# Linear attention with a gated feed-forward block: order of the first two token tiles' projections, and of the last tile's drains

## The chip, the cores and the metric

The kernel runs on one core of a Trainium2 chip. The metric is the device time of one execution in microseconds (us). The core's engines run their own instruction streams and wait for each other by semaphores: TensorE (PE in the profile, with its weight loads as PEld), VectorE (DVE), ScalarE (ACT), GpSimd (POOL), and SyncE (SP), which here issues the DMA transfers.

## The reference

For a sequence of S=2048 tokens of width D=576, with F=4608 and 32 heads of 18:

```python
def _A_ref(x, wqkv, wo):
    qkv = (x @ wqkv).reshape(B, S, 3, H, Dh).transpose(2, 0, 3, 1, 4)
    phi = lambda t: where(t > 0, t + 1, exp(t)) + 1e-6
    pq, pk = phi(q), phi(k)
    kv = einsum("bhsd,bhse->bhde", pk, v)
    z = einsum("bhsd->bhd", pk)
    o = einsum("bhqd,bhde->bhqe", pq, kv) / (einsum("bhqd,bhd->bhq", pq, z)[..., None] + 1e-6)
    return merge_heads(o) @ wo
xn = layernorm(x)
s = _A_ref(xn, wqkv, wo)
g = silu(gelu(xn @ w1 + b1) @ w2 + b2)
return x + s * g
```

All inputs are f32, and the kernel keeps f32 accuracy: every operand of a large product is split into a high part in the matmul's type (fp32r) and the low part that is left, and three products (high by high, high by low, low by high) are added.

## The kernel before

**Tiles.** 2048 tokens are 16 tiles of 128. The first phase handles them in pairs `(p, s)`: p is the pair, s its first or second tile. Pair 0 is called x8 and x12 here, after the names of the tiles, pair 1's first tile is `(1, 0)`. Each tile is loaded (`load_x`, L239), its mean and variance taken (`x_stats`, L244: two `bn_stats`, an aggregation and an addition on VectorE, a power on POOL, and, where ScalarE is to normalise, one more product on VectorE and on POOL), normalised (`x_norm`, L258: on ScalarE, or with `on_vector` on VectorE), and transposed by TensorE in five blocks into one PSUM buffer `pt` (`transpose_x`, L273). From there it is split: `x_hi` (L282, ScalarE casts it into `xH`, or for s=1 also into `x_tmp0h`/`x_tmp1h`), `x_lo` and `x_lo_tmp` (L293, L304: VectorE subtracts, into `xL` and `x_tmp0l`), and a raw copy is kept for later (`x_raw`, L290, ScalarE, into `rt` or `scr`).

**Weights.** The columns of `wqkv` for keys (1) and values (2) come in five slices of the contraction, k=0 to 4, of 288 KB each (`raw_w`, L533); slice 4, the rest, has 64 rows that are used as high and low part together. `Weight.split_k` (L159) lets ScalarE cast a slice to its high part and the engine that it is given (DV for VectorE, GP for POOL) subtract for the low part; `split_rest` and `split_v` do so for the rest and for the values.

**A projection.** `Plain` (L388) makes keys or values of one tile: 14 pairs of matmuls (each pair covers 2 x 288 columns): for k=0 to 3 the products number 3k (high by high), 3k+1 (low weights), 3k+2 (low x), and for the rest 12 and 13. `part(a, b)` issues a stretch of them. When the last is issued, ScalarE drains the two PSUM banks. K8 stands for the keys of x8, V8 for its values, and so on; in the profile both have the line L411 and the output `pl`, and their weights are `wkq_h`, `wkq_l`, `wkq_rh`, `wkq_rl` for keys, `wv_h`, `wv_l` for values.

**Order.** The start (L541 to L600) is recorded under `in_order()`, so each engine executes its instructions in the order in which they are written. The later pairs follow a plan of numbered times (`plan_pair`, L613), then come the projections that share sums of two tiles, the attention output, and the feed-forward phase. TensorE begins with 20 warm-up transposes (L453). Before, the order of projections is K8, V8, K12, V12. DMA issues go through SyncE's queue in written order.

**The tail.** `down_plain` (L1393) makes the last product of the feed-forward phase for the tiles 0 to 7 of the last group. Tiles 6 and 7 are halved by columns (`pd6a`, `pd6b`, `pd7a`, `pd7b`). Each half is drained by VectorE (`macc`, L1403), goes through silu on ScalarE (L1404), is multiplied (`xs`, L1356) and added to x (L1357), and stored. For tile 6's second half POOL does the last two, else VectorE.

Of the kernel before, what the change touches and what calls it, by code (L numbers as in the profile page):

```python
# [42 lines left out]
def linear_attention_gated_ffn(ctx, tc, x, wqkv, wo, w1, b1, w2, b2, out):  # L43
    nc = tc.nc
# [199 lines left out]
    def x_stats(p, s, first=False):  # L244
# [3 lines left out]
        nc.vector.bn_stats(st[:, 1, :], raw[:, HD:])  # L248
        mv = t1.tile([P, 4], F32, tag="mv", name=f"mv{p}{s}")
        nc.vector.bn_aggr(mv[:, 0:2], st)  # L250
        nc.vector.tensor_scalar_add(mv[:, 2:3], mv[:, 1:2], 1e-5)
        nc.gpsimd.tensor_tensor(mv[:, 3:4], mv[:, 2:3], nhalf, op=ALU.pow)
# [3 lines left out]
        stats[p, s] = mv  # L256

    def x_norm(p, s, on_vector=False):  # L258
        mv, raw = stats.pop((p, s)), xraw.pop((p, s))
# [128 lines left out]
    class Plain:  # L388


        def __init__(self, p, s, wk, dst, bias):
            cs = pair_cols(p)
            if s == 0:
                xk = [(xH[:, k, cs], xL[:, k, cs]) for k in range(4)] + [(xH[:, 4, cs],)]
            else:
                h, l = x_tmps[p % 2]
                xk = [(h[:, k], l[:, k]) for k in range(2)]
                xk += [(xH[:, 5 + k, cs], xL[:, 4 + k, cs]) for k in range(2)] + [(xH[:, 7, cs],)]
            self.seq = []
            for k in range(KT):  # L400
                h, l = xk[k][0], xk[k][-1]
                self.seq += [(h, 0, k), (h, 1, k)] + ([(l, 0, k)] if k < 4 else [])
            self.wk, self.dst, self.bias = wk, dst, bias
            self.ps = [bank(f"pl{p}{s}{n}")[:, :HD] for n in range(2)]

# [22 lines left out]
    def wv_part(hl, k, n):  # L428
        return (wv_h, wv_l)[hl][:, k, n * HD : (n + 1) * HD]

    def plain_k(p, s):
        return Plain(p, s, wk_part, k_ts[p % 2][s], one)

    def plain_v(p, s):
        return Plain(p, s, wv_part, v_t[s], None)
# [97 lines left out]
    def raw_w(which, between=None):  # L533
        raw, rest = w2p.tile([P, CF * D], F32, tag="w2r", name=f"raw{which}"), stage(D, f"rr{which}")
        for k in range(KT):
            dst = rest if k == 4 else raw[:, k * D : (k + 1) * D]
            nc.sync.dma_start(dst, wqkv[k, :, which * D : (which + 1) * D])
            if k == 2 and between:
                between()
        return raw, rest  # L540

    DV, GP = nc.vector, nc.gpsimd
    kt_raw = lambda raw, k: raw[:, k * D : (k + 1) * D]
    load_x(0, 0)
    raw_k, rest_k = raw_w(1, lambda: load_x(0, 1))
    x_stats(0, 0, True), x_norm(0, 0, True)
    wkq.split_k(0, kt_raw(raw_k, 0), DV)
    wkq.split_k(1, kt_raw(raw_k, 1), GP)
    transpose_x(0, 0)
    cs = pair_cols(0)  # L550
    nc.vector.tensor_copy(xH[:, 0:2, cs], pts[0, 0][:, 0:2])
    nc.vector.tensor_copy(xH[:, 2:5, cs], pts[0, 0][:, 2:])
    x_lo(0, 0)
    wkq.split_k(2, kt_raw(raw_k, 2), GP)
    wkq.split_k(3, kt_raw(raw_k, 3), DV)
    wkq.split_rest(rest_k, GP)
    raw_v, rest_v = raw_w(2, lambda: load_x(1, 0))
    load_x(1, 1)
    x_stats(0, 1, True), x_norm(0, 1, True)
    x_raw(0, 0)  # L560
    nc.gpsimd.memset(zacc, 0.0)

    N14 = 14
    plain_k(0, 0).part(0, N14)
    transpose_x(0, 1)
    split_v(0, kt_raw(raw_v, 0), DV)
    split_v(1, kt_raw(raw_v, 1), GP)
    x_hi(0, 1), x_lo_tmp(0), x_lo(0, 1)
    split_v(2, kt_raw(raw_v, 2), DV)
    split_v(3, kt_raw(raw_v, 3), GP)  # L570
    split_v(4, rest_v, DV)
    load_x(2, 0)
    load_x(2, 1)
    plain_v(0, 0).part(0, N14)
    x_stats(1, 0)
    x_raw(0, 1)
# [14 lines left out]
    s_hi(0), s_lo(0)  # L591
    x_store(0)
    plain_v(0, 1).part(0, N14)
    phi_exp(k_t[1], e_t[1])
    transpose_x(1, 1)
    x_hi(1, 1), x_lo_tmp(1), x_lo(1, 1)
    x_norm(2, 0)
# [754 lines left out]
        pair, src = tails["hs", b, f]  # L1352
        set_lo(pair, src, nc.vector)

    def gate_part(t, c, xt, s_t, cs, eng):
        eng.tensor_tensor(s_t[:, cs], c[:, cs], s_t[:, cs], op=MUL)  # L1356
        eng.tensor_tensor(s_t[:, cs], s_t[:, cs], xt[:, cs], op=ADD)  # L1357
        nc.sync.dma_start(out[t * P : (t + 1) * P, cs], s_t[:, cs])

# [33 lines left out]
    def down_plain(t, ws):  # L1393
# [226 lines left out]
```

## Time and profile before

| what | value |
|---|---|
| median of three runs | 1117.99 us (1117.21 to 1118.75) |
| the profiled execution, its own time | 1118.17 us |
| its span in the trace | 1116.4 us, 18757 instructions |
| TensorE busy | 1095.4 us, 98% of the span |
| VectorE, ScalarE, POOL busy | 812.6, 504.2, 466.1 us |
| granted TensorE clock, mean | 1.00 |
| DMA | 271.92 MB, mean 244 GB/s |
| first projection matmul | at 7.74 us |
| transposes of tile (1,0) | at 23.02 us |
| last matmuls begin | at 1109.85 us, for 0.56 |

The profile gives, in its rows, the start or the busy time of instructions by engine and line (L411 is line 411 of the kernel before), the output and the input of the operation, and behind them how long the engine sat idle and which engine's result ended it. A busy TensorE is not TensorE at its peak; the granted clock is given beside it in the windows.

### The profile page before, as it was taken

What the parts mean: (1) busy time and instruction counts of PE and PEld (TensorE: products, weight loads), DVE (VectorE), ACT (ScalarE), POOL (GpSimd) and SP (SyncE); (2) the same over time, 40 slices, a digit from 0 to 9 for tenths busy, and PEclk for the clock granted to TensorE, in tenths of its full rate; (3) what the DMA queues carried; (4) which work ended last, traced back from release to release, by engine and by line L of the source; (5) the groups of instructions that cost most, each with busy time, mean ns of one, the idle gap of its engine ahead of it and who ended that gap; (6) DMA issues with size and microseconds to landing.
All of it is one profiled execution on the core that took longest, in us unless ns stands there. A gap on an engine that the chain in (4) does not pass through costs nothing.

```text
span 1116.4 us, 18757 instructions
## 1 busy us (share of the span) xinstructions
PE 1095.4 (98%) x6924; PEld 1014.2 (91%) x6924; DVE 812.6 (73%) x1242; ACT 504.2 (45%) x913; POOL 466.1 (42%) x419
## 2 busy tenths in 40 slices
PE   8999999999999999999999999999999999999997
PEld 7899999999898898988989889899898998988987
DVE  6877667877688888888888887666475574664766
ACT  6766555554544444454443544424233243242351
POOL 5854433655354353543535433323224133242340
PEclk9999999999999999999999999999999999999999
DMA  5888747785988879588796869978766666766243
GB/s 203 301 261 280 253 135 224 250 285 188 358 270 308 265 236 355 177 296 272 229 357 185 288 235 382 359 252 282 225 204 213 214 200 216 226 200 218 85 142 114
DMA packets 95531, 271.92 MB, mean 244 GB/s; under 512 B 10381, under 2 KB 21133, under 8 KB 93391
## 3 DMA queue, kind: packets, MB, share of 16 engines
q1 hardware_dynamic: 90543, 260.68, 66.2%
q0 software_dynamic: 4896, 10.03, 5.3%
q8 instruction: 55, 0.90, 0.3%
q14 instruction: 37, 0.30, 0.1%
HBM read 165.94 MB, written 100.01 MB: 238 GB/s over the span
## 4 chain that ended last, share of the span: by engine, by line
PE 88%; DVE 4%; DMA 3%; ACT 2%; issue 1%; POOL 1%; SPq 0%; DVEq 0%; POOLq 0%; ACTq 0%
PE pm L1287 30%; PE e L1147 12%; PE a L1147 10%; PE zy L1147 10%; PE pl L411 5%; PE ps_s L894 5%; PE b L1147 4%; PE e L356 2%; DMA xH<-x_dram 2%; PE a L356 2%; PE z L356 2%; PE pd L1410 2%; PE ps_kva L464 1%; PE b L356 1%; DVE h_l L924 1%
## 5 line engine op out<-in xcount | busy, mean ns | idle before, releaser
L921 ACT CAST h_h<-g 128x512 fp32r<-128x512 f32 x204 | 120.1, 621 | 138.9 <-PE pm L1287 137.8
L924 DVE TENSOR_TENSOR h_l<-g,h_h 128x512 fp32r<-128x512 f32 x204 | 159.5, 782 | 0.0
L1295 DVE TENSOR_TENSOR macc<-macc,pm 128x576 f32<-128x576 f32 x128 | 96.2, 751 | 37.7 <-PE pm L1287 36.0
L1254 POOL TENSOR_TENSOR mid<-g 128x512 f32<-128x512 f32 x34 | 43.9, 1292 | 181.6 <-ACT g L1155 181.6
L1147 PE MATMUL a<-xH,wa 128*128 128x512 f32 x360 | 117.2, 390 | 0.5 <-DMA xH<-x_dram 0.5
L1297 DVE TENSOR_TENSOR macc<-pm,macc 128x576 f32<-128x576 f32 x90 | 68.2, 757 | 25.4 <-PE pm L1287 24.4
L1155 ACT ACTIVATE g<-b,b1c 128x512 f32<-128x512 f32 x36 | 24.8, 688 | 125.0 <-DVE b L1173 125.0
L1147 PEld LDWEIGHTS a<-xH,wa 128*128 128x128 f32 x360 | 67.6, 188 | 14.4 <-DMA xH<-x_dram 0.7
L1147 PE MATMUL e<-xSH,wb 128*128 128x512 f32 x216 | 66.6, 390 | 0.2 <-DVE b L1173 0.2
L1164 ACT COPY mid<-a 128x512 f32<-128x512 f32 x36 | 21.2, 588 | 91.2 <-PE a L1147 91.1
L1248 POOL TENSOR_TENSOR g<-g 128x512 f32<-128x512 f32 x34 | 49.5, 1456 | 22.2 <-DVE h_l L924 20.9
L1381 POOL TENSOR_TENSOR fin1l<-fin1h,fin1l 128x288 f32<-128x288 f32 x8 | 6.4, 805 | 121.9 <-DMA fin1l<-s_dram 63.0
L1147 PE MATMUL a<-xL,wa 128*128 128x512 f32 x144 | 56.2, 390 | 0.0
L1251 POOL TENSOR_TENSOR g<-g 128x512 f32<-128x512 f32 x34 | 49.9, 1467 | 13.1 <-DVE h_l L924 11.8
L1167 DVE TENSOR_TENSOR mid<-b,mid 128x512 f32<-128x512 f32 x36 | 24.6, 685 | 37.5 <-PE b L1147 37.4
L1147 PE MATMUL b<-xSH,w 128*128 128x512 f32 x144 | 50.2, 389 | 0.0
L1147 PE MATMUL zy<-xSH,w 128*128 128x512 f32 x144 | 50.2, 389 | 0.0
L1147 PE MATMUL e<-xSH,w 128*128 128x512 f32 x144 | 50.2, 389 | 0.0
L1147 PE MATMUL zy<-xH,w 128*128 128x512 f32 x144 | 50.2, 389 | 0.0
L1147 PEld LDWEIGHTS e<-xSH,wb 128*128 128x128 f32 x216 | 40.5, 188 | 9.0 <-DVE b L1173 0.6
L1245 POOL TENSOR_TENSOR g<-g 128x512 f32<-128x512 f32 x34 | 47.1, 1386 | 2.7
L1155 ACT ACTIVATE g<-e,b1c 128x512 f32<-128x512 f32 x36 | 24.8, 688 | 49.2 <-DVE e L1180 49.2
(932 smaller groups left out, 3594.2 us busy)
## 6 DMA issues: line engine op xcount, KB each, us to landing
op<-w SPq DMA_DIRECT2D x72, 256.0 KB
w<-op SPq DMA_DIRECT2D x72, 256.0 KB
w1raw<-w SPq DMA_DIRECT2D x18, 640.0 KB
w2raw<-w SPq DMA_DIRECT2D x10, 1152.0 KB
op_a<-wa SPq DMA_DIRECT2D x18, 640.0 KB
wa<-op_a SPq DMA_DIRECT2D x18, 640.0 KB
op<-w2o SPq DMA_DIRECT2D x19, 576.0 KB
w2r<-w SPq DMA_DIRECT2D x6, 1152.0 KB
```

Of the source, the lines that this page charges most:

```text
L356: nc.tensor.matmul(ps, st, mv, start=first and n == 0, stop=n == len(seq) - 1, skip_group_check=True,)
L411: nc.tensor.matmul(self.ps[n], st, self.wk(hl, k, n), start=(i == 0), stop=(i == n_all - 1))
L894: nc.tensor.matmul(self.ps[h], st[:, k, :], w[:, k, h * HD : (h + 1) * HD], start=(i == 0), stop=(i == len(self.seq) - 1),)
L921: nc.scalar.copy(pair[0], src)
L924: eng.tensor_tensor(pair[1], src, pair[0].bitcast(F32), op=SUB)
L1147: nc.tensor.matmul(ps.rearrange("p (c j) -> p c j", c=4), st, mv, start=first and n == 0, stop=n == len(seq) - 1, skip_group_check=True,)
L1155: nc.scalar.activation(g, ps, AF.Gelu_apprx_tanh, bias=b1c[:, f : f + 1])
L1248: tt(src[6, pr], src[5, pr], A(0, 0), op=ADD)
L1251: tt(src[3, pr], src[6, pr], A(0, 1), op=SUB)
L1287: nc.tensor.matmul(ps[:, q, :HD], hs[p][st][:, cs], m[:, p, :], start=(n == 0 and i not in CHAIN), stop=(n == len(seq) - 1), skip_group_ch ...
L1295: nc.vector.tensor_tensor(dst, dst, src, op=SUB)
L1297: nc.vector.tensor_tensor(dst, src, dst, op=ADD)
```

## The change

The sequence of the first two tiles is written anew, and in the tail the last tile's two halves are interleaved. No matmul is added or removed.

Loads: x12 is now the second transfer, ahead of all weights; the value slices and the tiles of pair 1 follow in the order of before. `x_stats` is divided in `x_bn` and `x_rstd`. x12 is normalised on ScalarE instead of VectorE, and with it come the one product on VectorE and the one on POOL. The first `xH` cast of slices 2 to 4 goes from VectorE to ScalarE; the low parts of k0 and k3 go from VectorE to POOL, those of k2 and the rest from POOL to VectorE. Projections come as K8, K12, V8, V12. K8 takes its 14 pairs in the order `FIRST`, and x12's transposes stand between its ninth and tenth pair; K12 takes them in the order `LATE`, with low x last. The exponential of tile 12's keys is issued before V12 instead of behind it.

```diff
-    def __init__(self, p, s, wk, dst, bias):
+    def __init__(self, p, s, wk, dst, bias, order=range(14)):
...
+        self.seq = [self.seq[i] for i in order]
...
+    FIRST = (0, 3, 2, 5, 6, 1, 8, 9, 4, 11, 7, 12, 10, 13)
+    LATE = (0, 1, 3, 4, 6, 7, 9, 10, 12, 13, 2, 5, 8, 11)
+    N14 = 14
     load_x(0, 0)
-    raw_k, rest_k = raw_w(1, lambda: load_x(0, 1))
-    x_stats(0, 0, True), x_norm(0, 0, True)
-    wkq.split_k(0, kt_raw(raw_k, 0), DV)
-    wkq.split_k(1, kt_raw(raw_k, 1), GP)
+    load_x(0, 1)
+    raw_k, rest_k = raw_w(1)
+    raw_v, rest_v = raw_w(2, lambda: load_x(1, 0))
+    load_x(1, 1)
+    x_bn(0, 0), x_rstd(0, 0, True)
+    x_bn(0, 1)
+    x_norm(0, 0, True)
+    x_rstd(0, 1)
+    wkq.split_k(0, kt_raw(raw_k, 0), GP)
     transpose_x(0, 0)
     cs = pair_cols(0)
     nc.vector.tensor_copy(xH[:, 0:2, cs], pts[0, 0][:, 0:2])
-    nc.vector.tensor_copy(xH[:, 2:5, cs], pts[0, 0][:, 2:])
+    wkq.split_k(1, kt_raw(raw_k, 1), GP)
+    nc.scalar.copy(xH[:, 2:5, cs], pts[0, 0][:, 2:])
     x_lo(0, 0)
-    wkq.split_k(2, kt_raw(raw_k, 2), GP)
-    wkq.split_k(3, kt_raw(raw_k, 3), DV)
-    wkq.split_rest(rest_k, GP)
-    raw_v, rest_v = raw_w(2, lambda: load_x(1, 0))
-    load_x(1, 1)
-    x_stats(0, 1, True), x_norm(0, 1, True)
+    x_norm(0, 1)
+    wkq.split_k(2, kt_raw(raw_k, 2), DV)
     x_raw(0, 0)
+    wkq.split_k(3, kt_raw(raw_k, 3), GP)
+    wkq.split_rest(rest_k, DV)
     nc.gpsimd.memset(zacc, 0.0)
-    N14 = 14
-    plain_k(0, 0).part(0, N14)
+    pr = plain_k(0, 0, FIRST)
+    pr.part(0, 9)
     transpose_x(0, 1)
+    x_hi(0, 1), x_lo_tmp(0), x_lo(0, 1)
     split_v(0, kt_raw(raw_v, 0), DV)
     split_v(1, kt_raw(raw_v, 1), GP)
-    x_hi(0, 1), x_lo_tmp(0), x_lo(0, 1)
+    pr.part(9, N14)
     split_v(2, kt_raw(raw_v, 2), DV)
     split_v(3, kt_raw(raw_v, 3), GP)
+    x_stats(1, 0)
+    plain_k(0, 1, LATE).part(0, N14)
     split_v(4, rest_v, DV)
     load_x(2, 0)
     load_x(2, 1)
-    plain_v(0, 0).part(0, N14)
-    x_stats(1, 0)
     x_raw(0, 1)
     for i in (3, 2, 1, 5, 4):
         x_sum(0, i, GP, xf(0, 1))
     k_t = k_ts[0]
     phi_exp(k_t[0], e_t[0])
     x_norm(1, 0)
-    plain_k(0, 1).part(0, N14)
+    plain_v(0, 0).part(0, N14)
+    phi_exp(k_t[1], e_t[1])
     transpose_x(1, 0)
...
     plain_v(0, 1).part(0, N14)
-    phi_exp(k_t[1], e_t[1])
     transpose_x(1, 1)
...
-        for k in range(2):
-            drain(k)
-            gate_part(*part(k))
+        drain(0), gate_mul(*part(0))
+        if t == 6:
+            gate_add(*part(0))
+        drain(1)
+        if t > 6:
+            gate_add(*part(0))
+        gate_mul(*part(1)), gate_add(*part(1))
```

In the last lines `gate_part` has been divided in `gate_mul` (the product) and `gate_add` (the sum and the store); tile 6 keeps its order.

ScalarE's order at the start, before (a name's number is that of its buffer; `raw_168` are the key slices, `raw_207` and `rr_208` the values', `pt_191` and `pt_262` the transposes of x8 and x12):

```order
L156 CAST wkq_h<-raw_168 128x2x288 x4
L167 CAST wkq_rh<-rr_169 128x576
L291 COPY rt<-pt_191 128x640
L420 ACTIVATE k_162<-pl_230,c_84 128x288
L420 ACTIVATE k_162<-pl_231,c_84 128x288
L438 CAST wv_h<-raw_207 128x576 x2
L287 CAST xH<-pt_262 128x384
L288 CAST x_tmp0h<-pt_262 128x256
L438 CAST wv_h<-raw_207 128x576 x2
L438 CAST wv_h<-rr_208 128x576
```

and with the change (`raw_170`, `raw_177`, `pt_209`, `pt_252` in the same roles; `xn_221` is x12 normalised):

```order
L156 CAST wkq_h<-raw_170 128x2x288 x2
L569 CAST xH<-pt_209 128x384
L274 ACTIVATE xn_221<-x_168,mv_201 128x576
L274 ACTIVATE xn_221<-x_168,mv_201 128x64
L156 CAST wkq_h<-raw_170 128x2x288
L298 COPY rt<-pt_209 128x640
L156 CAST wkq_h<-raw_170 128x2x288
L167 CAST wkq_rh<-rr_171 128x576
L294 CAST xH<-pt_252 128x384
L295 CAST x_tmp0h<-pt_252 128x256
L446 CAST wv_h<-raw_177 128x576 x2
```

The cast of xH's second part and x12's normalisation now stand between the casts of k1 and k2, the copy `rt` between k2 and k3, and x12's casts ahead of K8's drain.

VectorE's order in the same place, before (`mv` holds a tile's statistics):

```order
L264 TENSOR_SCALAR xn_184<-x_166,mv_180 128x576
L264 TENSOR_SCALAR xn_184<-x_166,mv_180 128x64
L157 TENSOR_TENSOR wkq_l<-raw_168,wkq_h 128x2x288
L551 CAST xH<-pt_191 128x256
L552 CAST xH<-pt_191 128x384
L297 TENSOR_TENSOR xL<-pt_191,xH 128x512
L301 TENSOR_TENSOR xH<-pt_191,xH 64x128
L157 TENSOR_TENSOR wkq_l<-raw_168,wkq_h 128x2x288
```

and with the change:

```order
L247 BN_STATS st_195<-x_168 128x6
L248 BN_STATS st_195<-x_168 128x6
L271 TENSOR_SCALAR xn_198<-x_166,mv_191 128x576
L271 TENSOR_SCALAR xn_198<-x_166,mv_191 128x64
L254 BN_AGGR mv_201<-st_195 128x2
L255 TENSOR_SCALAR mv_201<-mv_201 128x1
L258 TENSOR_SCALAR mv_201<-mv_201 128x1
L567 CAST xH<-pt_209 128x256
L304 TENSOR_TENSOR xL<-pt_209,xH 128x512
L308 TENSOR_TENSOR xH<-pt_209,xH 64x128
L157 TENSOR_TENSOR wkq_l<-raw_170,wkq_h 128x2x288
L168 TENSOR_TENSOR wkq_rl<-rr_171,wkq_rh 128x576
```

x12's statistics stand ahead of x8's normalisation, and the subtraction of k0 and the second cast of xH are gone from VectorE.

VectorE's end, before (`xs` holds a tile's product and sum):

```order
L1403 TENSOR_TENSOR macc<-pd7a,macc 128x288
L1356 TENSOR_TENSOR xs_11802<-macc,xs_11802 128x288
L1357 TENSOR_TENSOR xs_11802<-xs_11802 128x288
L1403 TENSOR_TENSOR macc<-pd7b,macc 128x288
L1356 TENSOR_TENSOR xs_11802<-macc,xs_11802 128x288
L1357 TENSOR_TENSOR xs_11802<-xs_11802 128x288
```

and with the change:

```order
L1420 TENSOR_TENSOR macc<-pd7a,macc 128x288
L1371 TENSOR_TENSOR xs_11804<-macc,xs_11804 128x288
L1420 TENSOR_TENSOR macc<-pd7b,macc 128x288
L1374 TENSOR_TENSOR xs_11804<-xs_11804 128x288
L1371 TENSOR_TENSOR xs_11804<-macc,xs_11804 128x288
L1374 TENSOR_TENSOR xs_11804<-xs_11804 128x288
```

The drain of the second half has passed the sum of the first.

More of the change, by code (lines that the diff above doesn't have):

```diff
@@ L242, in load_x, with x_bn @@
         nc.sync.dma_start(xraw[p, s], x[t * P : (t + 1) * P, :])
-    def x_stats(p, s, first=False):
+    def x_bn(p, s):
         st = t1.tile([P, 2, 6], F32, tag="st", name=f"st{p}{s}")
@@ L248, in x_stats, with x_rstd @@
         nc.vector.bn_stats(st[:, 1, :], raw[:, HD:])
+        stats[p, s] = st
+    def x_rstd(p, s, first=False):
+        st = stats[p, s]
         mv = t1.tile([P, 4], F32, tag="mv", name=f"mv{p}{s}")
@@ L256, in x_stats @@
         stats[p, s] = mv
+    def x_stats(p, s):
+        x_bn(p, s), x_rstd(p, s)
     def x_norm(p, s, on_vector=False):
@@ L429, in wv_part, with plain_k @@
         return (wv_h, wv_l)[hl][:, k, n * HD : (n + 1) * HD]
-    def plain_k(p, s):
-        return Plain(p, s, wk_part, k_ts[p % 2][s], one)
+    def plain_k(p, s, order=range(14)):
+        return Plain(p, s, wk_part, k_ts[p % 2][s], one, order)
     def plain_v(p, s):
@@ L1353, in tail_lo, with gate_mul, gate_add @@
         set_lo(pair, src, nc.vector)
-    def gate_part(t, c, xt, s_t, cs, eng):
+    def gate_mul(t, c, xt, s_t, cs, eng):
         eng.tensor_tensor(s_t[:, cs], c[:, cs], s_t[:, cs], op=MUL)
+    def gate_add(t, c, xt, s_t, cs, eng):
         eng.tensor_tensor(s_t[:, cs], s_t[:, cs], xt[:, cs], op=ADD)
```

## The prediction

> **What bounds the kernel now.** I read the chain of waits of the whole span first, by engine:
>
> ```profile
> PE 88%; DVE 4%; DMA 3%; ACT 2%; issue 1%; POOL 1%; SPq 0%; DVEq 0%; POOLq 0%; ACTq 0%
> ```
>
> TensorE carries 88% of what ended last, and the change takes no matmul away. It can only shorten stretches in which TensorE waits, and it touches two: the first 32 us and what follows the last matmul. Next the chain between 0 and 80 us, start, duration and count, for the price of TensorE's work where nothing holds it:
>
> ```profile
> 58.78 3.73 PE pl L411 x28
> 62.51 0.55 PE pt L277 x5
> ```
>
> One projection of a token tile (14 pairs of matmuls) is 3.73 us, 0.133 a matmul, and five transposes are 0.55. Then the timeline of TensorE at the start, of which these are the warm-up, the first pair and the transposes (start, duration, in brackets the idle time before and what ended it):
>
> ```profile
> 1.67 4.53 PE L453 MATMUL warm<-ident 128*128 128x128 f32 x20 [1.67 <-POOL ident masks.py:199]
> 6.36 0.77 PE L277 MATMUL pt<-ident,xn 128*128 128x128 f32 x5 [0.16 <-DVE xn L264]
> 7.74 0.51 PE L411 MATMUL pl<-wkq_h,xH 128*128 128x288 f32 x2 [0.61 <-ACT wkq_h L156]
> ...
> 13.26 0.74 PE L277 MATMUL pt<-ident,xn 128*128 128x128 f32 x5 [0.92 <-ACT k L420]
> ...
> 23.02 0.71 PE L277 MATMUL pt<-ident,xn 128*128 128x128 f32 x5
> ...
> 32.22 0.74 PE L277 MATMUL pt<-ident,xn 128*128 128x128 f32 x5 [0.52 <-DVE scr L317]
> ```
>
> From the first projection pair at 7.74 to the transposes of tile (1,0) at 23.02 there are 15.28 us. The work in it is K8, V8 and K12 (3 x 3.73) and five transposes (0.55): 11.74. So 3.54 us are lost. The table of windows gives that stretch 1.00 as TensorE's granted clock (third figure from the right) in spite of the waits:
>
> ```profile
> 7.74:23.02 15.28, 13.34 (x89) 11.98 (x90) 11.56 (x25) 9.38 (x18) 10.73 (x12) 1.00 0.66 250
> ```
>
> **The head, up to the first wait.** When weights land is told by the casts that wait for them, ScalarE's rows of L156:
>
> ```profile
> 4.84 0.67 ACT L156 CAST wkq_h<-raw 128x576 fp32r<-128x576 f32 x1 [2.75 <-DMA raw<-wqkv]
> 5.98 0.67 ACT L156 CAST wkq_h<-raw 128x576 fp32r<-128x576 f32 x1 [0.48 <-DMA raw<-wqkv]
> 7.02 0.67 ACT L156 CAST wkq_h<-raw 128x576 fp32r<-128x576 f32 x1 [0.36 <-DMA raw<-wqkv]
> 8.83 0.67 ACT L156 CAST wkq_h<-raw 128x576 fp32r<-128x576 f32 x1 [1.14 <-DMA raw<-wqkv]
> ```
>
> All these loads are 288 KB on one queue, so a slot is about 1.1 us, and x12 now sits unseen between 7.02 and 8.83. Moved to second place it takes the slot of 4.84; k0, k1, k2 come a slot later, about 5.98, 7.02 and 8.0; k3 and all behind it keep theirs. On VectorE this is the stretch that the change rewrites:
>
> ```profile
> 5.73 0.80 DVE L264 TENSOR_SCALAR xn<-x,mv 128x576 f32<-128x576 f32 x2 [0.75 <-POOL mv L252]
> 6.45 0.75 DVE L157 TENSOR_TENSOR wkq_l<-raw,wkq_h 128x576 fp32r<-128x576 f32 x1
> 7.17 0.42 DVE L551 CAST xH<-pt 128x256 fp32r<-128x256 f32 x1
> 7.51 0.55 DVE L552 CAST xH<-pt 128x384 fp32r<-128x384 f32 x1
> 8.09 0.69 DVE L297 TENSOR_TENSOR xL<-pt,xH 128x512 fp32r<-128x512 f32 x1
> ```
>
> The two statistics of x12, which read its 576 columns once as the normalisation does (0.8), go into the 0.75 hole ahead of x8's normalisation, which starts up to 0.07 later. If x12 landed a slot late, VectorE would stand there with the normalisation behind it, and 1.1 us would be lost; its slot speaks against that. x8's transposes and the cast at 7.17 move by as much; k0's subtraction no longer stands ahead of that cast, but three small operations for x12 do. k0's cast ends at 5.98+0.67=6.65 and k1's at 7.69, so the first pair starts at about 7.8 (7.74 before) and the second, k1's, at 8.07. Here the late slots cost nothing, because x8's transposes and cast run meanwhile; without that cover each tenth of lateness would count.
>
> ScalarE's prices stand in its rows of the next stretch:
>
> ```profile
> 19.38 0.70 ACT L418 COPY v<-pl 128x288 f32<-128x288 f32 x2 [2.73 <-PE pl L411]
> 19.96 0.71 ACT L291 COPY rt<-pt 128x640 f32<-128x640 f32 x1
> 20.55 0.80 ACT L442 ACTIVATE e<-k,c 128x576 f32<-128x576 f32 x1
> 21.23 1.20 ACT L267 ACTIVATE xn<-x,mv 128x576 f32<-128x576 f32 x2
> 23.09 0.89 ACT L420 ACTIVATE k<-pl,c 128x288 f32<-128x288 f32 x2 [0.67 <-PE pl L411]
> ...
> 29.46 0.42 ACT L288 CAST x_tmp1h<-pt 128x256 fp32r<-128x256 f32 x1
> ```
>
> Rows that follow each other start some 0.11 before the one ahead ends, so the steps are 0.58 (a drain of v), 0.59 (the copy rt), 0.68 (exponential) and 1.1 (normalisation).
>
> Behind k1's cast ScalarE now casts the second part of xH, 7.66 to 8.15 (0.5, a little under VectorE's 0.55); xL follows, 0.69, and TensorE waits until about 8.89 for the two xL pairs (8.83 before), done at 9.53. ScalarE normalises x12 from 8.05, about 1.1, then casts k2 (0.67): 9.82, and TensorE waits 0.32. Three pairs last to 10.76. ScalarE's copy rt and k3's cast end at 10.99: a wait of 0.26, two pairs, 11.66. The transposes of x12 end at 12.21, five more pairs at 13.54. The low halves are made beside this by POOL and VectorE. POOL's prices:
>
> ```profile
> 5.13 0.56 POOL L252 TENSOR_TENSOR mv<-mv,nhalf 128x1 f32<-128x1 f32 x1 [3.52 <-DVE mv L251]
> 6.74 3.12 POOL L157 TENSOR_TENSOR wkq_l<-raw,wkq_h 128x576 fp32r<-128x576 f32 x2 [1.04 <-ACT wkq_h L156]
> 10.33 1.43 POOL L168 TENSOR_TENSOR wkq_rl<-rr,wkq_rh 128x576 fp32r<-128x576 f32 x1 [0.47 <-ACT wkq_rh L167]
> ```
>
> POOL finishes x12's power and product near 7.6, k0's low half (1.4) near 9.0, k1's near 10.4 and k3's, from 11.0, near 12.45; TensorE asks for them near 10.2, 11.3 and 13.0. VectorE makes k2's low half by 11.1 (asked for at 12.5). The thinnest cover is the rest slice, now on VectorE. If that subtraction (0.75, as k0's at 6.45) is held by POOL's k3 until 12.4, it ends near 13.1; it is asked for at 13.27.
>
> **The head, from there on.** K12 and V8 follow without a hole: 13.54 + 3.73 + 3.73 = 21.0 for the transposes of (1,0), against 23.02. TensorE gains 2.02, or: 1.46 lost instead of 3.54, with a start 0.06 later. V's halves have the time of K12 to be made, which now stands ahead of V8, so they cost nothing; without this cover they would cost part of the 3.54. That (1,0) is normalised by then is the next cover: ScalarE must do it between K12's drain at 17.3 and 21.0. The next place where TensorE waits is the row of 32.22, behind the ScalarE list that ends in x_tmp1h. Before, from K12's drain at 23.09 to x_tmp1h's end at 29.88 are 6.79. Now the drain starts at about 17.3, and the rest slice's cast (0.58), V8's drain, rt, the exponential and the normalisation, 3.53 together, come behind it: 17.3+6.79+3.53=27.6, or 2.2 earlier than 29.88. The exponential of tile 12, moved up, is inside the 6.79 in both. The transposes at 32.22 come 2.34 after x_tmp1h, so now near 30.0, and TensorE by itself would be there at 21.0+0.55+3.73+0.55+3.73=29.56. ScalarE's list decides, with 2.2; TensorE's own gain is 2.0. I take **2.15**. From there every engine has the same instructions in the same order, and what is gained lasts to the end. The bounds: 1.3 (the first rival, below) and 2.5, if the last two waits of 0.32 and 0.26 and the thin covers cost nothing.
>
> **The tail.** The timeline of all engines after the last matmuls, tile 7's second half:
>
> ```profile
> 1109.85 0.56 PE L1423 MATMUL pd7b<-w__11748,xSL 128*128 128x288 f32 x3
> 1110.00 0.89 POOL L1357 TENSOR_TENSOR xs<-xs 128x288 f32<-128x288 f32 x1
> 1110.27 0.93 DVE L1357 TENSOR_TENSOR xs<-xs 128x288 f32<-128x288 f32 x1
> 1111.13 0.44 DVE L1403 TENSOR_TENSOR macc<-pd7b,macc 128x288 f32<-128x288 f32 x1
> 1111.60 0.44 ACT L1404 ACTIVATE macc<-macc 128x288 f32<-128x288 f32 x1 [2.04 <-DVE macc L1403]
> 1112.08 0.46 DVE L1356 TENSOR_TENSOR xs<-macc,xs 128x288 f32<-128x288 f32 x1 [0.51 <-ACT macc L1404]
> 1112.57 0.46 DVE L1357 TENSOR_TENSOR xs<-xs 128x288 f32<-128x288 f32 x1
> ```
>
> TensorE is done at 1110.41, but VectorE sits in the addition of the first half, 0.93 long beside POOL's (0.46 is the same addition at 1112.57), and drains the second only at 1111.13. Then drain, silu, product and sum follow each other with 0.03 to 0.04 between. The change drains first: 1110.45 instead of 1111.13, a gain of 0.68. The addition of the first half fits into the silu's time, 1110.9 to 1111.36, and the silu ends at 1111.37, so the product is hardly late: I take **0.65**. If the drain itself stood behind POOL's addition, to 1110.89, the gain would be 0.24: these are the bounds, 0.25 to 0.7. The first half's store goes out later than before, but ahead of the second's.
>
> **Sum.** 2.15+0.65=2.8: the profiled 1118.17 becomes 1115.4. The runs' median, 1117.99, is 0.18 lower, giving 1115.2; I say **1115.3**. The bounds add to 1.55 and 3.2, or 1116.6 and 1115.0 for the profiled run.
>
> **Rivals.** *ScalarE becomes the bound.* It gets x12's normalisation and a cast of xH ahead of k2 and k3. If its five steps between 7.66 and 11.0 go by their full durations (0.11 more each, 0.55), and TensorE restarts late after each of its waits (0.37 for a first pair in place of 0.27 is in the sum already; the same again is 0.3), the head gains 1.3 and the time is 1118.17-1.3-0.65=1116.2. For it speaks that two of TensorE's waits now hang on ScalarE's list; against it, that ScalarE has over 2 us of spare time before K12's drain.
>
> *The tail gives next to nothing*: 1118.17-2.15-0.25=1115.8. POOL's addition slowing VectorE's to twice its time speaks for it. Against it speaks xL at 8.09, which like the drain reads one operand from PSUM: beside POOL's subtraction from 6.74 it took 0.69 for 512 columns, no more than 0.75 for the 576 of k0 without POOL.
>
> *The change does not do what it says*: the gain of the head is lost where DMA stores run between 32 and 60 us, whose position in the queue moves less. With the tail alone 1117.5, with neither 1118.0. Against it speaks that the chain between 58.78 and 62.51 is TensorE's own work, without a transfer between.
>
> *Slower: TensorE's clock falls.* The 20 warm-up transposes took 4.53 us, 0.227 each; five later ones take 0.55, 0.11 each. At the start TensorE thus runs at half rate, and a run of 4.5 us was needed before the full one. The first tile is now broken by waits of 0.55, 0.32 and 0.26. If these drop the rate from 8.9 on, seven pairs up to 11.0 last 1.9 longer, and 4.5 us of the unbroken run behind them do 2.25 less: 4.15 in all, and 1118.17-2.8+4.15=1119.5. It decides as soon as the matmul pairs after 8.9 follow at 0.53 instead of 0.27. Against it: the wait of 0.92 at 13.26 changed nothing before, with a clock of 1.00. The Trainium skill, page "TensorE: Matmul & The Clock Gate", section "A second HAM failure mode: psum-queue depth-cycling", tells of a kernel whose TensorE idled briefly and often, and whose clock swung between half and full; by that rule this rival would come true, while the 1.00 over a stretch with 3.5 us of waits does not agree.
>
> **Chances.** The forecast 0.66, with its own range 1114.6 to 1116.1; ScalarE 0.17; the tail 0.05; no effect 0.05; slower 0.07. About 0.2%, or 2.24 us, can be told from no change: faster means under 1115.75. That takes 0.56 of the forecast, 0.03 of ScalarE's case and 0.02 of the tail's: 0.61 faster. Slower 0.07, same 0.32. The range, with the runs' spread of 0.8 to either side, is 1114.2 to 1117.3; above it lie the slower case and most of no effect.
>
> **What would show it.** The first pair at 7.8, the k2 pair near 9.85, x12's transposes near 11.7, those of (1,0) at 21.0, and those of tile (2,0) near 30.0 instead of 32.22; each with its waits named after ScalarE. In the tail the drain of 7b within 0.05 of the last matmul's end. A first projection spread beyond 13.9, a wait for wkq_rl, or V8 with holes would break the head's sum; a drain that starts late, the tail's; pairs at 0.53 would show the clock.

## The result, and the profile after

The changed kernel takes 1115.09 us (median of 12 runs, 1114.35 to 1116.54); the kernel before, run beside it, 1117.93. The ratio is 0.9973, with a 95% interval of 0.9964 to 0.9982: 2.84 us faster, where 2.8 and 1115.3 had been forecast. The profiled execution took 1115.12 (span 1113.3), 3.05 less than that of before. In the experiments below one run each of the head alone, of the cast on VectorE and of some groups of the kernel before took far longer; the medians count them (at most 0.08 by it), the ratios leave them out.

The chain of waits of the changed kernel, by engine, gives TensorE 2% more of the span than before, and transfers 1% instead of 3%:

```profile
PE 90%; DVE 3%; ACT 3%; issue 2%; DMA 1%; POOL 0%; SPq 0%; DVEq 0%; POOLq 0%; ACTq 0%
```

TensorE's timeline at the start, the rows that answer to those of before (L419 are projections, L284 transposes):

```profile
7.71 1.09 PE L419 MATMUL pl<-wkq_h,xH 128*128 128x288 f32 x4 [0.61 <-DVE xH L567]
9.37 0.80 PE L419 MATMUL pl<-wkq_h,xL 128*128 128x288 f32 x4 [0.57 <-DVE xL L304]
10.30 0.53 PE L419 MATMUL pl<-wkq_h,xH 128*128 128x288 f32 x2
...
12.11 0.71 PE L284 MATMUL pt<-ident,xn 128*128 128x128 f32 x5
...
21.45 0.71 PE L284 MATMUL pt<-ident,xn 128*128 128x128 f32 x5
...
30.66 0.73 PE L284 MATMUL pt<-ident,xn 128*128 128x128 f32 x5 [0.30 <-DVE scr L324]
```

The first pair starts where it started before (7.74), and the transposes of tile (1,0) come at 21.45 instead of 23.02, those of (2,0) at 30.66 instead of 32.22: the head gains 1.56 in this execution. The window over the same stretch as before is 13.74 long, with TensorE busy for 12.86 at the full granted clock (first and second figure, and third from the right):

```profile
7.71:21.45 13.74, 12.86 (x89) 11.93 (x90) 9.17 (x17) 11.76 (x23) 11.15 (x11) 1.00 0.73 278
```

The end, all engines, answers to the seven rows of before:

```profile
1107.45 0.56 PE L1440 MATMUL pd7b<-w__11750,xSL 128*128 128x288 f32 x3
1107.59 0.89 POOL L1374 TENSOR_TENSOR xs<-xs 128x288 f32<-128x288 f32 x1
1108.05 0.46 DVE L1420 TENSOR_TENSOR macc<-pd7b,macc 128x288 f32<-128x288 f32 x1 [0.22 <-PE pd7b L1440]
1108.43 0.45 DVE L1374 TENSOR_TENSOR xs<-xs 128x288 f32<-128x288 f32 x1
1108.54 0.44 ACT L1421 ACTIVATE macc<-macc 128x288 f32<-128x288 f32 x1 [1.37 <-DVE macc L1420]
1109.02 0.46 DVE L1371 TENSOR_TENSOR xs<-macc,xs 128x288 f32<-128x288 f32 x1
1109.51 0.46 DVE L1374 TENSOR_TENSOR xs<-xs 128x288 f32<-128x288 f32 x1
```

The second half is drained at 1108.05, 0.04 after the last matmuls end, beside POOL's addition and in its usual 0.46. From the last matmul's start to the last sum's end are 2.52 us (1107.45 to 1109.97), before 3.18 (1109.85 to 1113.03): the tail gains 0.66.

Head and tail make 2.22 of the 3.05 of this pair of executions. Laid side by side, instruction by instruction, the two traces differ by about 1.5 to 1.9 from 30 us to 648 us, and by 2.4 from 700 us on. Most of this step, 0.66, is one wait, which the profile of before shows in TensorE's timeline behind the reload of the normalised tokens, and which is absent after:

```profile
699.86 0.51 PE L1147 MATMUL a<-xH,wa 128*128 128x512 f32 x1 [0.50 <-DMA xH<-x_dram]
```

In before this matmul starts 0.79 behind the one ahead of it, in after 0.13.

### The profile page after: what moved, and what is told of

Read it like the earlier page. It is cut to its first block, busy times and chain, and to the rows that moved or that the text cites. A ratio compares the mean times of both kernels' runs of the same rounds, so it can differ in the third digit from the quotient of the medians.

```text
span 1113.3 us, 18759 instructions
## 1 busy us (share of the span) xinstructions
PE 1094.0 (98%) x6924; PEld 1013.6 (91%) x6924; DVE 811.5 (73%) x1240; ACT 505.6 (45%) x916; POOL 467.2 (42%) x420
## 4 chain that ended last, share of the span: by engine, by line
PE 90%; DVE 3%; ACT 3%; issue 2%; DMA 1%; POOL 0%; SPq 0%; DVEq 0%; POOLq 0%; ACTq 0%
PE pm L1302 32%; PE e L1162 12%; PE a L1162 10%; PE zy L1162 10%; PE ps_s L909 5%; PE pl L419 5%; PE b L1162 4%; PE e L363 2%; PE a L363 2%; PE z L363 2%; PE pd L1427 2%; PE ps_kva L472 1%; PE b L363 1%; DVE h_l L939 1%; PE ptp L877 1%
```

## The experiments

Times are medians, the ratio is that to the kernel before on the same chip, with its interval. The kernel before, run beside them, had medians of 1118.07 (tail, head and reload), 1117.71 (values first, order of the pairs, x12 late and the first of the faster heads), and 1117.95 (the rest). An interval is about 0.1%, or 1 us, to either side: it separates the larger effects, and the smaller ones are read in the traces.

**The tail alone, and the head alone.** The first is the kernel before with the new order of drains, the second the changed kernel with the old one.

```diff
-        for k in range(2):
-            drain(k)
-            gate_part(*part(k))
+        drain(0), gate_mul(*part(0))
+        if t == 6:
+            gate_add(*part(0))
+        drain(1)
...
```

> The kernel before with the new order of tile 7's drains alone. My theory (drain first gains 0.66, the rest of the change's 2.84 comes from ahead of it): 0.66 us faster than before, 1117.3 beside 1117.93, with the drain of pd7b within 0.05 of the last matmul's end. Rival (the store of the first half, issued later, holds the end): no gain. Up to the tail this is the kernel before, so its trace also tells whether TensorE's wait for the reload of xH near 700 us (0.50 in before, none in after) belongs to before: if it does, it stands here again with 0.4 to 0.8; if it is chance, anything from 0 to 0.8.

> The changed kernel with the old order of the drains. Theory: the head gives 1.56 (the difference of the transposes of tile (2,0): 32.22 before, 30.66 after), and the tail's 0.66 is missing. If the wait for the reload of xH near 700 us is gone because of the head, the time is 1115.09+0.66=1115.75, or 2.2 under before; if that wait comes and goes by chance, the time is 1117.93-1.56=1116.4 in the median and the wait stands in this trace in some runs.

The tail alone: 1117.18, ratio 0.9988 (0.9976 to 0.9999). That is 0.89 under the 1118.07 beside it, and the tail's 0.66 fits. The head alone: 1115.44, ratio 0.9973 (0.9963 to 0.9984), 2.63 under the same, so nearer to the first of its two theories than to the second. Its trace shows a head that is better than that of the changed kernel's profile, though the instructions there are the same:

```profile
7.66 0.76 PE L419 MATMUL pl<-wkq_h,xH 128*128 128x288 f32 x4 [0.61 <-DVE xH L567]
8.81 0.79 PE L419 MATMUL pl<-wkq_h,xL 128*128 128x288 f32 x4 [0.38 <-DVE xL L304]
...
20.88 0.71 PE L284 MATMUL pt<-ident,xn 128*128 128x128 f32 x5
...
30.09 0.74 PE L284 MATMUL pt<-ident,xn 128*128 128x128 f32 x5 [0.30 <-DVE scr L324]
```

30.09 against 32.22 is a gain of 2.13, within 0.02 of the forecast's 2.15. The difference to 30.66 begins with the first key slice. ScalarE's rows, the head alone:

```profile
5.38 0.67 ACT L156 CAST wkq_h<-raw 128x576 fp32r<-128x576 f32 x1 [3.29 <-DMA raw<-wqkv]
6.27 0.67 ACT L156 CAST wkq_h<-raw 128x576 fp32r<-128x576 f32 x1 [0.22 <-DMA raw<-wqkv]
7.55 0.48 ACT L569 CAST xH<-pt 128x384 fp32r<-128x384 f32 x1 [0.61 <-DVE xH L567]
```

and in the changed kernel's profile:

```profile
6.73 1.49 ACT L156 CAST wkq_h<-raw 128x576 fp32r<-128x576 f32 x2 [4.64 <-DMA raw<-wqkv]
8.12 0.47 ACT L569 CAST xH<-pt 128x384 fp32r<-128x384 f32 x1
8.49 1.20 ACT L274 ACTIVATE xn<-x,mv 128x576 f32<-128x576 f32 x2
9.59 0.66 ACT L156 CAST wkq_h<-raw 128x576 fp32r<-128x576 f32 x1
```

The same slice, behind the same two transfers, landed at 5.38 in one execution and at 6.73 in the other. Where it is late, ScalarE still has both weight casts to do when x8's transposes are there, the second cast of xH starts 0.57 later (8.12, 7.55), and with it xL and x12's normalisation, k2 and k3. It also explains why the first four matmuls last 1.09 there and 0.76 in the head alone: the two of the second pair wait for k1's cast, which ends at 8.22. TensorE's weight loads in the changed kernel's profile show it:

```profile
8.27 0.30 PEld L419 LDWEIGHTS pl<-wkq_h,xH 128*128 128x128 f32 x2 [0.29 <-ACT wkq_h L156]
```

**The reload.** In both kernels the reload of xSH was put behind that of xH, since TensorE reads it 1.5 us later.

```diff
-                for k, at in ((2, 12), (3, 12), (1, 13), (0, 13)):
+                for k, at in ((3, 12), (1, 13), (0, 13), (2, 13)):
```

> The kernel before with only the order of the four reloads for the second half of the tokens changed: xSH, which TensorE reads 1.5 us later than xH, goes last instead of ahead of xL and xH. Theory (before pays some 0.6 for a late xH near 700 us, in most of its runs): 0.5 to 0.7 faster than before, no wait at that place. Rival (the wait is a chance of the one profiled run): within 0.2 of before.

> The changed kernel with the same reordering of the reloads. Theory (after has no wait there, since its transfers ahead of the reload ran sooner): within 0.2 of the changed kernel, 1115.1. Rival (the wait comes in some runs of both): 0.2 to 0.4 faster than the changed kernel.

Before with this order: 1117.55, ratio 1.0000 (0.9990 to 1.0009); the wait is gone from its trace (0.13 between the two matmuls). After with it: 1114.98, ratio 0.9969 (0.9957 to 0.9980). The first has a median 0.52 under the 1118.07 beside it, but its ratio shows no gain; the interval is too wide to exclude 0.6, so the times don't settle how often the wait comes. The traces say more. Up to there the tail alone is the kernel before, and in the table of its waits the same wait (of the weight loads, total, times, longest) is half as long as in before, where it was 0.7:

```profile
PEld a L1147 <- DMA xH<-x_dram: 0.3, 1, 0.3
```

Of the other kernels that keep the old order of reloads and come to that place at about the same time as before, one has 0.07 there and one none; five that come there earlier have none, nor have two that come later. The wait is real, but its size goes by the run; 0.66 is what this pair of profiles has of it, and nothing here shows that the change removes it.

**Values first.** The changed kernel with V8 ahead of K12, and the values' rest slice ahead of the statistics of (1,0).

```diff
-    x_stats(1, 0)
-    plain_k(0, 1, LATE).part(0, N14)
     split_v(4, rest_v, DV)
+    x_stats(1, 0)
+    plain_v(0, 0).part(0, N14)
...
-    plain_v(0, 0).part(0, N14)
+    plain_k(0, 1, LATE).part(0, N14)
```

> The changed kernel with V8 ahead of K12 again, all else of the head kept. Theory (K12 ahead of V8 is the cover under which the value slices are split): V8 starts where K12 did, near 13.4 to 14.0, and waits for the low halves, which in the changed kernel end near 15.5 (slice 0), 16.2 (slice 1), 17.0 (slice 2) and 18.7 (slice 3) against 13.7, 14.5, 15.3 and 16.1 for asked: about 1.5 to 2.0 us lost, 1116.6 to 1117.1, holes in V8 named after the splits. Rival (the order of K8's pairs and x12's early normalisation carry the gain): 1115.1 to 1115.5.

1117.38, ratio 0.9997 (0.9988 to 1.0006), apart from the changed kernel's interval: the gain of the head is gone. TensorE's timeline has V8 with holes, and (1,0) back where it was before:

```profile
14.97 0.53 PE L419 MATMUL pl<-wv_l,xH 128*128 128x288 f32 x2 [0.78 <-DVE wv_l L447]
...
16.26 0.52 PE L419 MATMUL pl<-wv_l,xH 128*128 128x288 f32 x2 [0.23 <-POOL wv_l L447]
...
23.04 0.71 PE L284 MATMUL pt<-ident,xn 128*128 128x128 f32 x5
```

Here k0 landed early (5.42), x12's transposes came at 11.54, and all the rest of the change was in place. So the cover of K12 over the value slices is what the head's gain needs; the other edits alone don't bring it.

**The order of the pairs.** K8 and K12 take their pairs from 0 to 13.

```diff
-    pr = plain_k(0, 0, FIRST)
+    pr = plain_k(0, 0)
...
-    plain_k(0, 1, LATE).part(0, N14)
+    plain_k(0, 1).part(0, N14)
```

> The changed kernel with K8's and K12's pairs in the order of before (0 to 13), x12's transposes still behind the ninth pair. Theory (the order by readiness lets TensorE work while POOL makes the low halves of k0 and k1): k0's low half is there near 9.0 and k1's near 10.4, so the second pair waits until 9.0 and the fifth until 10.4; x12's transposes come 0.5 to 0.8 later than 11.6, and the time is 0.4 to 0.8 above the changed kernel, 1115.5 to 1115.9. Rival (the order matters little, since the same halves are asked for in the end): within 0.2 of 1115.1.

1115.97, ratio 0.9980 (0.9971 to 0.9989): 0.9 above the changed kernel in the median, which the intervals do not separate. The second pair does wait for POOL's low half of k0, as expected, and K8 is later by it:

```profile
9.15 0.53 PE L419 MATMUL pl<-wkq_l,xH 128*128 128x288 f32 x2 [0.92 <-POOL wkq_l L157]
9.83 0.53 PE L419 MATMUL pl<-wkq_h,xL 128*128 128x288 f32 x2 [0.15 <-DVE xL L304]
...
22.89 0.77 PE L284 MATMUL pt<-ident,xn 128*128 128x128 f32 x5 [0.71 <-ACT xn L274]
```

But x12's transposes stand at 12.20, only 0.09 behind those of the changed kernel's profile, whose k0 had landed as late. So the median is near the theory's, but not by the theory's way. The rest of its loss in this trace comes with a wait of 0.26 for k3's low half and, in the last row, one of 0.71 for the normalisation of (1,0), which was not expected; what makes that late is told below. What the order by readiness is worth by itself is not shown.

**x12 late.** x12 is loaded behind k2 again, its statistics, normalisation and transposes put where it can be had then.

```diff
-    load_x(0, 1)
-    raw_k, rest_k = raw_w(1)
+    raw_k, rest_k = raw_w(1, lambda: load_x(0, 1))
...
-    x_bn(0, 1)
     x_norm(0, 0, True)
-    x_rstd(0, 1)
...
-    x_norm(0, 1)
     wkq.split_k(2, kt_raw(raw_k, 2), DV)
     x_raw(0, 0)
+    x_bn(0, 1), x_rstd(0, 1)
     wkq.split_k(3, kt_raw(raw_k, 3), GP)
     wkq.split_rest(rest_k, DV)
+    x_norm(0, 1)
...
-    pr.part(0, 9)
+    pr.part(0, N14)
...
-    pr.part(9, N14)
```

> The changed kernel with x12 loaded behind k2 as before, its statistics behind the subtraction of k2 on VectorE, its normalisation behind all key casts on ScalarE, and its transposes behind all 14 pairs of K8. Theory (early x12 saves the hole between x12's transposes and the casts that K12 waits for): K8 ends near 11.9 to 12.4, transposes follow, and K12 waits some 0.9 for the casts: 0.4 to 0.9 above the changed kernel, 1115.5 to 1116.0. Rival (x12's early load costs as much as it saves, since every key slice comes a slot later and ScalarE casts k2 behind x12's normalisation): the same or up to 0.4 faster than the changed kernel.

1119.39, ratio 1.0013 (1.0004 to 1.0022): slower than before, by far more than expected. The hole for K12's casts is there with 0.95, but the loss begins earlier. VectorE's normalisation of x8, two instructions:

```profile
5.70 2.96 DVE L271 TENSOR_SCALAR xn<-x,mv 128x576 f32<-128x576 f32 x2 [0.75 <-POOL mv L256]
```

and POOL at the same time:

```profile
5.65 2.97 POOL L157 TENSOR_TENSOR wkq_l<-raw,wkq_h 128x576 fp32r<-128x576 f32 x2
```

k0 had landed at 4.35, a slot earlier, so POOL's subtractions of k0 and k1 could start just ahead of the normalisation, which took 2.96 instead of the 0.80 of before. That puts the first pair at 9.66 instead of 7.71, and TensorE had little to do meanwhile. The table of windows gives it 1.29 us of work in the 3.41 us up to 8.97, and behind that a granted clock of 0.50 (third figure from the right) until 15.80:

```profile
5.56:8.97 3.41, 1.29 (x9) 0.72 (x7) 2.96 (x2) 0.67 (x1) 3.06 (x3) 1.00 1.01 358
9.66:15.80 6.14, 6.14 (x24) 5.77 (x24) 3.56 (x9) 3.98 (x7) 2.62 (x4) 0.50 0.92 341
```

The pairs follow at 0.48 there, instead of 0.27. In this kernel that costs little: the pair that needs k3's low half starts at 15.85, just behind POOL's subtraction (14.39 to 15.80), which had stood behind x12's late power in POOL's queue, so at full clock TensorE would have waited for it. To try what the normalisation does, k0's low half was given back to VectorE:

```diff
-    wkq.split_k(0, kt_raw(raw_k, 0), GP)
+    wkq.split_k(0, kt_raw(raw_k, 0), DV)
```

> As x12_late, but k0's low half is subtracted by VectorE, behind x8's normalisation, so that POOL has nothing to do while x8 is normalised. In x12_late the two instructions of that normalisation took 2.96 us together instead of 0.81, beside POOL's subtractions of k0 and k1 (5.65 to 8.62). Theory (the two engines hold each other up there): the normalisation takes 0.8 again, x8's transposes start near 6.4 instead of 7.4 and 8.7, and some 2.0 to 2.6 us come back; what remains above the changed kernel, 0.5 to 1.3, is what x12's late load costs: 1115.7 to 1116.5. Rival (the normalisation was late for another reason, a late landing or the clock): at most 0.5 faster than x12_late.

The normalisation is 0.80 long again:

```profile
5.62 0.80 DVE L271 TENSOR_SCALAR xn<-x,mv 128x576 f32<-128x576 f32 x2 [0.75 <-POOL mv L256]
```

but the time, 1119.11 (ratio 1.0007, 0.9997 to 1.0017), is 0.3 lower only, which the intervals do not separate. In the trace x12's transposes do come back by 2.04 (14.45, from 16.49). TensorE's rows there:

```profile
13.81 0.53 PE L419 MATMUL pl<-wkq_l,xH 128*128 128x288 f32 x2 [1.81 <-POOL wkq_l L157]
14.45 0.71 PE L284 MATMUL pt<-ident,xn 128*128 128x128 f32 x5
16.11 0.55 PE L419 MATMUL pl<-wkq_h,x_tmp0h 128*128 128x288 f32 x2 [0.95 <-ACT x_tmp0h L295]
```

POOL made k3's low half (12.37 to 13.77) only after x12's power, which stood ahead of it in its queue. Behind these waits the clock falls here too. The pairs from 16.48 to 19.81 follow at 0.48, which makes them about 1.5 us longer, and the transposes of (1,0) stand at 25.19, only 0.51 ahead of those with the long normalisation:

```profile
16.40:19.80 3.40, 3.40 (x16) 3.40 (x16) 3.35 (x6) 1.94 (x4) 2.52 (x2) 0.51 0.52 208
```

That the two engines hold each other up is shown by this pair; what the early load of x12 is worth by itself is not, since both kernels also lose by POOL's queue, and the second by the fallen clock.

**A faster head.** First, xL in two halves, the casts of k2 and k3 ahead of x12's normalisation, the raw copy of x8 on VectorE, and ten pairs ahead of x12's transposes.

```diff
-    x_lo(0, 0)
-    x_norm(0, 1)
+    for a in (0, 2):
+        nc.vector.tensor_tensor(
+            xL[:, a : a + 2, cs], pts[0, 0][:, a : a + 2], xH[:, a : a + 2, cs].bitcast(F32), op=SUB
+        )
...
-    x_raw(0, 0)
     wkq.split_k(3, kt_raw(raw_k, 3), GP)
+    nc.vector.tensor_copy(xf(0, 0), pts[0, 0])
+    x_norm(0, 1)
```

> The changed kernel with the head's two waits attacked: xL made in two halves, the first right behind the first cast of xH, so that the two xL pairs need not wait; the casts of k2 and k3 ahead of x12's normalisation on ScalarE; the raw copy of x8 on VectorE; k1's low pair behind x12's transposes, which now follow ten pairs. Theory (ScalarE's list between 7.5 and 11 and the one xL subtraction set K8's end): x12's transposes at 10.8 to 11.2 instead of 11.6, those of (1,0) 0.4 to 0.7 earlier than 20.9, the time 1114.4 to 1114.7. Rival (POOL's low halves or the landing of k2 and k3 set it): within 0.2 of 1115.1.

1114.70, ratio 0.9971 (0.9960 to 0.9982). The time is within what was expected, the way is not: x12's transposes came at 12.01, and waited 0.42 for the copy that had been given to VectorE:

```profile
9.51 1.50 DVE L157 TENSOR_TENSOR wkq_l<-raw,wkq_h 128x576 fp32r<-128x576 f32 x1
11.04 0.82 DVE L578 COPY rt<-pt 128x640 f32<-128x640 f32 x1
```

Ahead of it VectorE's subtraction of k2 took 1.50, beside POOL's three (7.59 to 12.29). Then the second cast of xH alone went back to VectorE:

```diff
-    nc.scalar.copy(xH[:, 2:5, cs], pts[0, 0][:, 2:])
+    nc.vector.tensor_copy(xH[:, 2:5, cs], pts[0, 0][:, 2:])
```

> The changed kernel with the second cast of xH back on VectorE. Theory (that cast stands on ScalarE behind the casts of k0 and k1, whose landing moves by over 1 us from run to run, 5.38 to 6.73, and with it xL and all that follows): xL starts near 8.1 however late k0 lands, where it started at 8.63 in the profiled run with k0 at 6.73; median 0.1 to 0.4 faster than the changed kernel, with the transposes of (1,0) at 20.6 to 20.9. Rival (k2's cast behind x12's normalisation decides in any case): the same within 0.1.

1115.66, ratio 0.9970 (0.9958 to 0.9981): no gain. xL does start at 8.01 and x12's transposes stand at 11.32, earlier than in any trace so far, but (1,0) is late. VectorE's value subtractions in this kernel, and the statistics of (1,0) behind them:

```profile
14.05 3.95 DVE L447 TENSOR_TENSOR wv_l<-raw,wv_h 128x576 fp32r<-128x576 f32 x2
17.93 0.45 DVE L247 BATCH_NORM_STATS2 st<-x 128x6 f32<-128x288 f32 x1
```

and TensorE's wait that comes of it:

```profile
21.65 0.77 PE L284 MATMUL pt<-ident,xn 128*128 128x128 f32 x5 [0.70 <-ACT xn L274]
```

The same two subtractions take 0.76 and 1.27 in the changed kernel's profile:

```profile
14.73 0.76 DVE L447 TENSOR_TENSOR wv_l<-raw,wv_h 128x576 fp32r<-128x576 f32 x1
16.14 1.27 DVE L447 TENSOR_TENSOR wv_l<-raw,wv_h 128x576 fp32r<-128x576 f32 x1 [0.64 <-ACT wv_h L446]
```

There VectorE's first started ahead of POOL's (14.73, 14.83), and POOL's took 1.96; here POOL's was ahead by 0.01 (14.04, 14.05), and VectorE's first took 2.04. Whichever starts first goes on, and the other stands. The late (1,0) with the pairs in order has the same cause: POOL's started at 14.92, VectorE's at 15.13, and the two took 1.83 and 2.01. So the statistics were put ahead of them:

```diff
+    x_stats(1, 0)
     split_v(2, kt_raw(raw_v, 2), DV)
     split_v(3, kt_raw(raw_v, 3), GP)
-    x_stats(1, 0)
```

> As cast_dve, but with the statistics of tile (1,0) ahead of the third and fourth value slice on VectorE and POOL. In cast_dve VectorE's two value subtractions took 3.95 us together beside POOL's, the statistics behind them came at 17.93, ScalarE's normalisation waited 0.88 for POOL, and the transposes of (1,0) 0.70 for it, at 21.65. Theory (that wait ate what the earlier xL had gained): no such wait, the transposes of (1,0) near 20.6 to 20.9, and the median 0.4 to 0.8 under cast_dve's 1115.66, 1114.9 to 1115.3. Rival (cast_dve is above the changed kernel for another reason): no gain over cast_dve, or a wait for a value slice in V8 in place of the other.

The wait is gone and (1,0) stands at 20.82, with k0 as late as 6.51:

```profile
20.82 0.71 PE L284 MATMUL pt<-ident,xn 128*128 128x128 f32 x5
```

The median is 1114.92, 0.74 under the kernel that it was made from, but on another chip, and the ratios to before show no gain of one over the other (here 0.9976, 0.9967 to 0.9985; there 0.9970). So only the trace shows the cause; that the time gains by it is not shown. Last, a kernel with the cast on VectorE, k2 and k3 cast ahead of x12's normalisation, ten pairs ahead of x12's transposes, and the new order of reloads:

```diff
-    x_norm(0, 1)
     wkq.split_k(2, kt_raw(raw_k, 2), DV)
     x_raw(0, 0)
     wkq.split_k(3, kt_raw(raw_k, 3), GP)
+    x_norm(0, 1)
...
```

> Together: the second cast of xH on VectorE; on ScalarE the casts of k2 and k3 ahead of x12's normalisation; ten pairs of K8 ahead of x12's transposes, with k1's low pair behind them; and the reload of xSH behind xH. Theory: x12's transposes at 10.9 to 11.2 instead of 11.6, those of (1,0) at 20.2 to 20.5 instead of 20.9, no wait at the reload: 0.5 to 0.9 faster than the changed kernel, 1114.2 to 1114.6. Rival (the low halves of k2 and the rest, VectorE's, are held up by POOL's three subtractions, which now follow each other without a gap): within 0.3 of the changed kernel, with waits named after VectorE.

1114.82 (1114.73 to 1114.93 in six runs), ratio 0.9963 (0.9950 to 0.9977): the best ratio of all, 0.27 under the changed kernel's median, which is less than the intervals can separate. The rival was right in the size, and in that VectorE's subtraction of k2, 0.76 elsewhere, was held by POOL:

```profile
9.02 1.99 DVE L157 TENSOR_TENSOR wkq_l<-raw,wkq_h 128x576 fp32r<-128x576 f32 x1
10.40 0.30 PEld L419 LDWEIGHTS pl<-wkq_h,xH 128*128 128x128 f32 x2 [0.33 <-ACT wkq_h L156]
```

It is not what put x12's transposes at 11.44, though. The subtraction ends at 11.0, and the pair that needs it starts at 11.06, some 0.02 late. The longer wait, in the second row, is for ScalarE's cast of k3, which ended at 10.35: it stands behind the copy rt, and that had waited 0.50 for VectorE.

## Why the prediction held, step by step

- **The bound.** TensorE's waits at the start and behind the last matmul were the right two places; both shrank.
- **The head's 2.15.** Over the traces with this head the transposes of (2,0) stand at 30.66, 30.09 and 30.17 (the last with the reload's new order), against 32.22, 32.59 and 32.12 for the old head: 2.0 in the mean, 1.56 in the profiled pair. (The 32.59 begins with x8's transposes, which took 1.24 instead of 0.77 in that execution.) The step that was mis-sized is the slot: "k0, k1, k2 come a slot later, about 5.98, 7.02 and 8.0". k0 landed anywhere from 5.38 to 6.73, and the sentence that late slots cost nothing holds only for the early end of that. In the late case ScalarE's casts of k0 and k1 hold the cast of xH, and the sum loses 0.6. With that cast on VectorE the xL pairs came at 8.72 though k0 landed at 6.40 and 6.51 (the last two kernels above), so it is ScalarE's list that makes the lateness count.
- **The waits in K8.** Forecast were 0.55, 0.32 and 0.26 ahead of the xL pairs, k2 and k3; in the trace of the head alone these three come at 8.81, 9.74 and 10.91, forecast at 8.89, 9.85 and 11.02.
- **The thin covers.** The rest slice's subtraction on VectorE was indeed held by POOL's k3, 1.51 long, and ended 0.18 before it was asked for. The other, (1,0)'s normalisation, held in the changed kernel, and broke in the traces of two experiments with a wait of 0.7: the forecast had it as a cover and named neither its margin nor what could take it. The margin was as thin: the first and longer of its two instructions ended at 21.27, 0.18 ahead of the transposes.
- **V8 behind K12** cost nothing, as said; with V8 first, the head's gain is lost.
- **The next wait.** (2,0) waits 0.30 instead of 0.52, and the name is VectorE's. ScalarE's list up to x_tmp1h gave 30.0 (its own terms add to 27.62, or 2.26 earlier), the traces with an early k0 30.09 and 30.17. The size held, but the path is another: before, VectorE waited 0.51 for x_tmp1h; now it goes from one of its own operations (xSL, which ends at 28.32) to the next without a wait, and the last that it had waited for ScalarE is the copy `scr`, at 24.77. The rows of before and after:

```profile
29.91 0.42 DVE L305 TENSOR_TENSOR x_tmp1l<-pt,x_tmp1h 128x256 fp32r<-128x256 f32 x1 [0.51 <-ACT x_tmp1h L288]
28.35 0.42 DVE L312 TENSOR_TENSOR x_tmp1l<-pt,x_tmp1h 128x256 fp32r<-128x256 f32 x1
```

- **The tail's 0.65** was 0.66, with the drain 0.04 behind the last matmul. The drain was not held by POOL's addition, so the lower bound, 0.25, did not come. One reading in the argument against that bound was wrong: k0's subtraction at 6.45 was not without POOL, whose own ran from 6.74 on; VectorE's had started first, like the 0.76 at 14.73 above.
- **What was not in the sum** is the wait at the reload, 0.66 between the two profiled executions. There it makes up for the 0.6 by which the head fell short. The total of the profiled pair agrees with the forecast partly by luck, because these two errors cancel. Whether that of the medians does too is open: by medians the tail alone gives 0.89 and the head alone 2.63, 3.5 together against 2.84 for both, each with an interval of about 1.
- **The rivals.** ScalarE as the bound came in part, in executions where k0 lands late, but for another reason than its step lengths. The clock did not fall in the changed kernel: from 9.37 on the pairs follow at 0.27, or 0.37 behind a wait. The rival was no idle one, though: in both kernels with x12 late the granted clock fell to half, and in the second about 1.5 us were lost by it. Its price was built on a run of 4.5 us at half rate; in the changed kernel the warm-up's step went from 0.21 to 0.11 already 2.8 us after its start.

## What to carry to other kernels

When an engine waits for prepared operands, put work whose operands are ready, or are made soonest, ahead of it as cover: here a whole projection on weights that were already split. An edit that is costed at nothing because of cover should be given its margin in time and the engine that can eat it; in the traces of two variants TensorE waited 0.7 where the margin had been 0.18. When a variant is slower than its waits explain, look at the granted clock. A profile of one execution says what waits there are, not how often: a second trace of the same instructions, which experiments on another part give for nothing, tells the two apart.

## What the runs showed of the hardware

VectorE and POOL hold each other up, by whole instructions, in some of their work from SBUF. VectorE's subtraction of two SBUF operands (576 columns) took 0.75 or 0.76 alone and up to 2.04 beside POOL's, its normalisation (one tensor and two scalars per row, two instructions) 0.80 alone and 2.96. The statistics, with one SBUF operand, were not held: 0.45 and 0.44 beside POOL's subtraction (17.33 and 17.70 in the changed kernel). Those with one operand in PSUM were not held: xL took 0.69 beside POOL's subtraction, before and after, the drain of the tail 0.46 beside POOL's addition, where the addition of two SBUF operands had taken 0.93. The Trainium skill, page "SBUF — State Buffer", section "Who interferes with whom", gives just this rule, an exclusive lock on a port pair that the two engines share; the traces agree with it. What was not foreseen is that a shift of 0.1 in which of the two starts first changes an instruction's length from 0.8 to 2.0, and with it what stands behind.

The landing of a transfer near the start moves from run to run: the first key slice, as third transfer of the queue, landed at 5.38, 5.42, 5.72, 5.94, 6.40, 6.51, 6.58, 6.61 and 6.73 in nine executions; as second, at 4.33 to 4.84 in five.

The granted clock of TensorE fell to 0.50 behind stretches with little work: in one kernel with x12 late behind 3.41 us with 1.29 of work, for 6.8 us, in the other behind waits of 1.81 and 0.95, for 3.4 us. A wait of 0.92 in before, with 2.23 of work in the 3.40 us around it (11.40 to 14.80), left it at 1.00. Where between these the limit lies is not shown.
